# Batch 1's v pooled on GpSimd, and its scores issued in two groups ahead of all its values

## The chip, the cores and the metric

The kernel runs on one core of a Trainium2 chip. The metric is the device time of one execution in microseconds (us), the median of several runs; lower is better. A profile is one further execution, recorded by the hardware profiler: for every instruction it gives the engine, the start, the duration and what released it. PE is TensorE, DVE is VectorE, ACT is ScalarE, POOL is GpSimd, and SP is the engine whose queue starts transposes by DMA and the stores.

## The reference, cut to what matters

Attention over pooled keys and values, followed by an MLP whose activation is `h * cos(h)`:

```python
k_p = k.reshape(B, H, Sp, 8, D).mean(axis=3)          # 576 rows -> 72
v_p = v.reshape(B, H, Sp, 8, D).mean(axis=3)
attn = softmax(q @ k_p.T / sqrt(D))
x = (attn @ v_p)  -> [4608 tokens, 512]               # B=8, H=8, S=576, D=64
h = x @ w_in                                          # 512 -> 2048
out = (h * cos(h)) @ w_out                            # 2048 -> 512
```

All inputs and the output are fp32; the kernel computes in bf16 with fp32 accumulation.

## The kernel before, in words

The 4608 tokens are cut into nine tiles of 512. Tile t has an *up stage* (64 matmuls of 512 columns for h, in eight steps `fp` of 8 matmuls; ACT takes the cosine of each step, DVE multiplies it with h into `g_sb`) and a *down stage* (g times w_out). In tile 0 the down stage is 64 plain matmuls of 512 columns, numbered n = 0 to 63 in an order written out by hand; from tile 1 on it is seven products of 256 columns, built from sums and differences of g (g1 to g4, made by DVE) and of w_out (w1 to w4, made once by `put_weights`). A token tile isn't a batch: a batch has 576 rows, so tile 0 needs the first 512 rows of batch 0, and tile 1 the last 64 of batch 0 and 448 of batch 1. The attention of batch b = t+1 is therefore put between the matmuls of tile t, and its result xT must be there when the up stage of tile t+1 starts.

A manual schedule holds: every engine runs its instructions in the order of the program, and Tile adds the semaphores. So the order of the Python calls is the order on each engine[...].

What the change touches in tile 0:

- **Loads** are issued by POOL's queue, in program order (lines 508 to 522). After batch 0 come w_in 0 to 2, k of batch 1, the first half of q, w_in 3, the second half of q, w_out 0, v, and w_out 2, 1, 3. Batch 1's k and v lie in one staging tile of `kv_st` (two slots), in the *even* layout: 128 partitions with 9 rows each. From batch 2 on, k and v have a layout of their own, 72 partitions with 8 rows of each head, one for each pooled row.
- **Pooling.** In the even layout PE pools with a 0/1 matrix `groups`: `pool_k_mm` (line 170), and `pool_v_mm` (line 181), 18 matmuls and one DVE copy into `vz`, the weights of the values. In the 72-partition layout POOL adds rows: `pool_first` (line 152), four instructions of two heads each into `half_sums`, and `pool_rest` (line 158), two more and a last one into `vz`, or two last ones into `ring` for k.
- **q** is transposed for batch 0 and 1 on PE (`q_transpose_mm`, line 208), 18 blocks, and copied from PSUM by DVE or ACT (line 215).
- **Scores and values.** Batch 1 is cut into four units `us[0..3]`: 256 rows and four heads each, units 0 and 1 for heads 0 to 3, units 2 and 3 for heads 4 to 7. `REST` is the last 64 rows of the batch before, all heads. `scores` is a group of matmuls (line 233) and an exponential on ACT (line 240). `values` (line 262) is a group of matmuls (line 268), then on ACT two logarithms of the sums (line 274) and one exponential (line 275), and then two multiplications on DVE into xT (line 279), which may be put off through a list `later`. These use three PSUM pairs `banks[0..2]`; in tile 0 step fp of the up stage uses `banks[fp % 3]`.
- **The order in the down stage of tile 0** is the list `fill` (line 614): pairs of a matmul number n and what is issued ahead of it.
- **Weights.** `put_weights(i, engine, ks)` (line 381) makes w1 to w4 for half i. DVE makes w1 of half 0 at n = 4, w3 of half 1 at n = 36, and w2 and w4 of half 1 at the end of the stage; POOL makes the others after it has issued the loads of batch 2.
- **Tile 1** needs batch 2: its q and its pooled k are transposed by DMA (`q_transpose`, `k_transpose`, lines 204 and 190, on SP's queue) before the scores, `vz` before `values_rows` (line 287), and the rows of x go through a DMA transpose (line 304) into xT.

In tiles 7 and 8 there is no next batch (`steady` is false). There `reads[1]` takes product 1 out of its PSUM bank (line 447), and product 3 writes that bank again.

The softmax here doesn't subtract the row's maximum and nothing guards it: scores larger than these inputs give would overflow.

## Time and profile before

| | us |
|---|---|
| runs | 286.9, 287.76, 288.06; median 287.76 |
| the profiled execution, device time | 287.52 |
| its span, first to last instruction | 285.7 |
| PE busy | 275.0 (96%) |
| DVE busy | 215.1 |
| ACT busy | 164.2 |
| POOL busy | 144.2 |
| start until tile 0's up stage | 0 to about 16.8 |
| tile 0, up stage | 16.8 to 33.0 |
| tile 0, down stage | 33.0 to 52.65 |
| tile 1 | 52.65 to 83.12 |
| tile 2, as an example of the steady tiles | 83.12 to 112.1 |

Times in the text are from the start of the span. In the chain of work that ended last, each row is a start, a duration and what was at work; a row of DVE, ACT or DMA between rows of PE is a place where PE followed that engine. In the timeline, a row is a start, a duration, the engine, the line of the kernel, the operation, output <- input with partitions x elements, a count, and, in brackets, how long the engine sat idle before and what released it. A duration of merged rows runs from the first start to the last end. The granted clock of TensorE was 0.998, and a matmul of 512 columns was started every 0.216 us (24 of them between 52.65 and 57.83).

### The profile page before, as it was taken

How to read it: one execution, taken by the hardware profiler on the slowest of the kernel's cores; microseconds unless marked ns; L12 is line 12 of the kernel's file. 1: busy time of each engine (PE TensorE's matmuls, PEld its weight loads, DVE VectorE, ACT ScalarE, POOL GpSimd, SP SyncE). 2: the span in 40 equal slices, each digit the busy share in tenths (PEclk: the TensorE clock that was granted, in tenths of full speed). 3: DMA queues.
4: the chain of work that ended last, by engine and by line, in shares of the span. 5: the costliest groups of instructions: out<-in, count | busy, mean ns of one | idle time of the engine just before them, and what ended most of it. 6: DMA issues, size and time to landing. Idle time of an engine off the chain costs nothing.

```text
span 285.7 us, 5835 instructions
## 1 busy us (share of the span) xinstructions
PE 275.0 (96%) x2338; PEld 176.4 (62%) x2360; DVE 215.1 (75%) x314; ACT 164.2 (57%) x193; POOL 144.2 (50%) x150
## 2 busy tenths in 40 slices
PE   7889999999999999999999999999999999999994
PEld 2645554446864697458745874587458845874683
DVE  6458747899947995799569956995699569747972
ACT  3886798367147735773567456745665566337600
POOL 8553079995799359925992499349900000000000
PEclk9999999999999999999999999999999999999999
DMA  7999999795789987897789868882660261015014
GB/s 156 204 207 206 207 205 217 123 181 74 125 109 137 169 172 119 127 179 147 111 135 160 173 97 150 156 176 41 124 147 9 52 137 29 2 36 111 2 37 110
DMA packets 57737, 36.12 MB, mean 126 GB/s; under 512 B 35440, under 2 KB 53360, under 8 KB 57712
## 3 DMA queue, kind: packets, MB, share of 16 engines
q0 software_dynamic: 19744, 18.07, 41.1%
q1 hardware_dynamic: 37328, 17.18, 29.8%
q10 hardware_dynamic: 640, 0.52, 0.8%
q8 instruction: 18, 0.29, 0.4%
q14 instruction: 7, 0.06, 0.1%
HBM read 36.70 MB, written 9.44 MB: 161 GB/s over the span
## 4 chain that ended last, share of the span: by engine, by line
PE 80%; DVE 9%; DMA 3%; ACT 3%; issue 2%; POOL 0%; DVEq 0%; POOLq 0%; ACTq 0%
PE bank L353 35%; PE obank L431 27%; PE obank L370 4%; PE obank L353 4%; DVE g_sb L367 3%; PE bank L233 3%; DVE g L397 3%; DMA q_b<-in_q_dram 2%; ACT cos L363 2%; PE bank L295 2%; DMA xT<-x_rows 1%; PE bank L268 1%; DVE w L387 1%; PE bank L431 1%; ACT ex L240 1%
## 5 line engine op out<-in xcount | busy, mean ns | idle before, releaser
L353 PE MATMUL bank<-xT,w_in_sb 128*128 128x512 bf16 x495 | 113.1, 379 | 1.7 <-DMA xT<-x_rows 0.6
L363 ACT ACTIVATE cos<-bank,half_pi 128x1024 f32<-128x1024 f32 x64 | 70.3, 1113 | 57.7 <-PE bank L353 55.8
L353 PEld LDWEIGHTS <-w_in_sb 128*128 128x128 bf16 x576 | 56.0, 98 | 67.0 <-issue 1.7
L367 DVE TENSOR_TENSOR g_sb<-bank,cos 128x1024 bf16<-128x1024 f32 x64 | 77.3, 1220 | 25.8 <-ACT cos L363 25.6
L156 POOL TENSOR_TENSOR half_sums<-kv_st 72x512 f32<-72x512 bf16 x48 | 54.8, 1167 | 0.7 <-issue 0.2
L240 ACT ACTIVATE ex<-bank 72x1024 bf16<-72x1024 f32 (+1 forms) x40 | 35.0, 928 | 33.9 <-PE bank L233 33.8
L431 PEld LDWEIGHTS <-g 128*128 128x128 bf16 x512 | 47.9, 98 | 7.0 <-issue 1.2
L431 PE MATMUL obank<-w,g 128*128 128x256 bf16 x368 | 42.8, 272 | 0.3 <-DVE p_sb L445 0.2
L431 PEld LDWEIGHTS <-g_sb 128*128 128x128 bf16 x384 | 36.7, 98 | 6.8 <-DVE g_sb L367 0.2
L162 POOL TENSOR_TENSOR half_sums<-half_sums 72x512 f32<-72x512 f32 x24 | 30.4, 1288 | 0.1
L431 PE MATMUL obank<-w_out_sb,g_sb 128*128 128x256 bf16 x240 | 28.8, 273 | 0.0
L397 DVE TENSOR_TENSOR g<-g_sb 128x1024 bf16<-128x1024 bf16 x32 | 23.2, 725 | 0.5
L712 POOL COPY gate<-g 1x1 bf16<-1x1 bf16 x5 | 0.9, 180 | 36.9 <-DVE g L397 36.9
L279 DVE TENSOR_TENSOR xT<-bank,inv 64x256 bf16<-64x256 f32 x14 | 5.9, 422 | 15.1 <-ACT inv L275 15.1
L300 DVE TENSOR_TENSOR x_rows<-bank,inv_rows 128x512 bf16<-128x512 f32 x24 | 16.6, 692 | 0.8
L431 PE MATMUL obank<-w_out_sb,g 128*128 128x256 bf16 x112 | 15.6, 273 | 0.0
L431 PE MATMUL obank<-w,g_sb 128*128 128x256 bf16 x128 | 15.3, 273 | 0.0
L353 PE MATMUL obank<-xT,w_in_sb 128*128 128x512 bf16 x64 | 15.1, 379 | 0.0
L370 PE MATMUL obank<-w_out_sb,g_sb 128*128 128x512 bf16 x61 | 14.7, 379 | 0.4 <-issue 0.3
L233 PE MATMUL bank<-qT,kk 64*72 64x128 bf16 (+2 forms) x288 | 12.8, 221 | 0.1
L233 PEld LDWEIGHTS <-kk 64*72 64x72 bf16 x288 | 8.9, 110 | 5.3 <-issue 3.8
L331 ACT ACT_TABLE_LOAD x9 | 11.5, 1283 | 0.9 <-PEq L730 0.7
(103 smaller groups left out, 276.9 us busy)
## 6 DMA issues: line engine op xcount, KB each, us to landing
out_dram<-o_two SPq DMA_DIRECT2D x64, 128.0 KB, 2.4
kv_st<-in_v_dram POOLq DMA_DIRECT2D x8, 576.0 KB, 11.3
kv_st<-in_k_dram POOLq DMA_DIRECT2D x7, 576.0 KB, 8.3
q_b<-in_q_dram POOLq DMA_DIRECT2D x6, 576.0 KB, 7.7
w_in_sb<-in_moe_w_in_dram POOLq DMA_DIRECT2D x4, 512.0 KB, 13.4
w_out_sb<-in_moe_w_out_dram POOLq DMA_DIRECT2D x4, 512.0 KB, 18.5
q_b<-in_q_dram POOLq DMA_DIRECT2D x4, 288.0 KB, 12.0
g_sb<-in_k_dram SPq DMA_DIRECT2D x1, 576.0 KB, 3.5
```

Source lines behind the costliest of these rows:

```text
L156: nc.gpsimd.tensor_tensor(out=s[:, h:h + 2], in0=x[:, h:h + 2, 0:4, :], in1=x[:, h:h + 2, 4:8, :], op=ADD)
L162: add(out=s[:, h:h + 4, 0:2, :], in0=s[:, h:h + 4, 0:2, :], in1=s[:, h:h + 4, 2:4, :], op=ADD)
L233: nc.tensor.matmul(pair[:Sp, bank, c:c + n].rearrange("p (g n) -> p g n", n=64), lhsT=kk[b % 2][half[r], key_slot(b, h0 + i, r), 0:Sp], rh ...
L240: nc.scalar.activation(out=ex[:, 0:nh * n].rearrange("p (a n) -> p a n", a=2), in_=pair[:Sp, :, 0:nh * n // 2], func=ACTF.Exp, scale=scale ...
L300: nc.vector.tensor_tensor(out=x[0:n].rearrange("p (j a d) -> p j a d", j=KCH, a=2), in0=ps[0:n, :, 0:2 * (D + 2)].rearrange("p j (a w) -> ...
L331: nc.scalar.preload_act_table_set("natural_log_exp_and_others")
L353: nc.tensor.matmul(h[j] if h is obanks else h[:, j, :], lhsT=w_in_sb[fc // 4][:, ki, (fc % 4) * 128:(fc % 4 + 1) * 128], rhs=xT[:, ki, t * ...
L363: nc.scalar.activation(out=c, in_=ps, func=ACTF.Sin, bias=half_pi[:, :1])
L367: nc.vector.tensor_mul(out=o, in0=ps, in1=c)
L370: nc.tensor.matmul(o, lhsT=g_sb[:, fc, ms * 128:(ms + 1) * 128], rhs=w_out_sb[fc // 4][:, fc % 4, :], start=(fc == 0), stop=(fc == FFCH - 1))
L397: nc.vector.tensor_tensor(out=out[:, f0:f1], in0=x, in1=y, op=op)
L431: mms.append(lambda bank=bank, first=first, g=g, w=w, fc=fc, p=p: nc.tensor.matmul(bank[p], lhsT=g(fc, p), rhs=w(fc), start=(first and fc ...
```

## The change

In tile 0:

1. v of batch 1 is loaded in the 72-partition layout, in two DMAs of four heads: one into the second half of batch 1's staging tile, one into the memory of g1, which is otherwise written from tile 1 on. POOL pools it (`pool_first`, `pool_rest`), right after it has issued the loads of k and q of batch 2, and ahead of v of batch 2 and of its `put_weights`. The 18 matmuls and the copy of `pool_v_mm` go.
2. The second half of q of batch 1 is loaded after w_out 2, and its 9 blocks are transposed in the down stage ahead of n = 15 (`late_q`) instead of in step 6 of the up stage. Both copies are DVE's.
3. In `fill`, the scores of REST and of units 0 and 1 come together at n = 8, then the values of REST; the scores of units 2 and 3 together at n = 16; the values of units 0, 1 and 2 together at n = 24, their multiplications at n = 32; the values of unit 3 at n = 44 (before: 40).
4. DVE makes w1 of half 0 after step 5 of the up stage instead of at n = 4.

Elsewhere: in tile 1, POOL issues the next load of k after `pool_rest` of k instead of ahead of it; in tiles 7 and 8, `reads[1]` comes ahead of g3 and g4 of the second half.

```diff
@@ -109,12 +109,16 @@
     def q_tile(b):
         staged["q", b] = qst.tile([128, KCH, ROW, D], BF16, name="q_b", tag="q_b")
 
-    def load_kv(b, which, src):
-
-        st = kv_tile()[:Sp, 0:H * POOL * D].rearrange("p (h t d) -> p h t d", h=H, t=POOL)
-        nc.gpsimd.dma_start(out=st.rearrange("p h t d -> p h (t d)"),
-                            in_=src[b].rearrange("h (p t) d -> p h (t d)", t=POOL))
-        staged[which, b] = st
+    def load_kv(b, which, src, homes=None):
+
+        homes = homes or [kv_tile()]
+        n = H // len(homes)
+        staged[which, b] = []
+        for i, home in enumerate(homes):
+            st = home[:Sp, 0:n * POOL * D].rearrange("p (h t d) -> p h t d", h=n, t=POOL)
+            nc.gpsimd.dma_start(out=st.rearrange("p h t d -> p h (t d)"),
+                                in_=src[b, i * n:(i + 1) * n].rearrange("h (p t) d -> p h (t d)", t=POOL))
+            staged[which, b] += [st[:, h:h + 2] for h in range(0, n, 2)]
 
     def load_q(b):
         q_tile(b)
@@ -151,9 +155,8 @@
 
     def pool_first(b, which):
 
-        x, s = staged.pop((which, b)), half_sums
-        for h in range(0, H, 2):
-            nc.gpsimd.tensor_tensor(out=s[:, h:h + 2], in0=x[:, h:h + 2, 0:4, :], in1=x[:, h:h + 2, 4:8, :], op=ADD)
+        for i, x in enumerate(staged.pop((which, b))):
+            nc.gpsimd.tensor_tensor(out=half_sums[:, 2 * i:2 * i + 2], in0=x[:, :, 0:4, :], in1=x[:, :, 4:8, :], op=ADD)
 
     def pool_rest(b, which):
 
@@ -505,21 +508,27 @@
     half_pi = consts.tile([128, 1], FP32, name="half_pi")
     nc.vector.memset(half_pi, math.pi / 2.0)
 
-    kv_even_tiles(1)
+    st = kv_tile()
+    staged["k", 1] = even_part(st, 0)
     q_tile(1)
     for cg in range(3):
         load_w_in(cg)
     load_even(staged["k", 1], 1, k)
     load_even(staged["q", 1], 1, q, 0, 2)
     load_w_in(3)
-    load_even(staged["q", 1], 1, q, 2, 4)
     load_w_out(0)
-    load_even(staged["v", 1], 1, v)
+    load_kv(1, "v", v, [st[:, KCH * ROW * D:], g1.rearrange("p f n -> p (f n)")])
     nc.gpsimd.memset(vz[1], float(POOL))
     for i in range(2):
         nc.gpsimd.memset(ring[i], 0.0)
-    for cg in (2, 1, 3):
+    load_w_out(2)
+    load_even(staged["q", 1], 1, q, 2, 4)
+    for cg in (1, 3):
         load_w_out(cg)
+    load_kv(2, "k", k)
+    load_q(2)
+    pool_first(1, "v")
+    pool_rest(1, "v")
 
     def warm_up(n, bank):
 
@@ -570,13 +579,14 @@
             if t == 0:
                 if fp == 4:
                     puts = pool_k_mm(1, obanks[0], 0, 2), pool_k_mm(1, obanks[1], 2, 4)
-                elif fp in (5, 6):
-                    g0 = 9 * (fp - 5)
-                    puts = q_transpose_mm(1, obanks[0], g0, g0 + 5), q_transpose_mm(1, obanks[1], g0 + 5, g0 + 9)
-                if fp in (4, 5, 6):
+                elif fp == 5:
+                    puts = q_transpose_mm(1, obanks[0], 0, 5), q_transpose_mm(1, obanks[1], 5, 9)
+                if fp in (4, 5):
                     puts[0](vec)
                     between = ((puts[1], act),)
             up_g(t, fp, between)
+            if t == 0 and fp == 5:
+                put_weights(0, nc.vector, (1,))
             if 0 < t and 3 <= n < 6:
                 put_gs(*[(k, 0) for k in (((3,), (1,), ()) if t == 1 else ((1, 2), (3,), (4,)))[n - 3]])
             if 0 < t and b < B:
@@ -606,15 +616,29 @@
         def V_(n, bank, wait=None):
             return lambda: values(b, us[n], banks[bank], wait)
 
+        def scores_of(*parts):
+            for part in parts:
+                scores_mm(*part)
+            for part in parts:
+                scores_exp(*part)
+
+        def late_q():
+            for put in [q_transpose_mm(1, banks[0][:, i, :], g0, g1) for i, g0, g1 in ((0, 9, 14), (1, 14, 18))]:
+                put(vec)
+
+        def muls():
+            while later:
+                later.pop(0)()
+
         fill = []
         if t < B:
             exp_tables()
             fill = [(1, lambda: scores(t, REST, banks[2])), (16, lambda: values(t, REST, banks[1]))]
         if t == 0:
-            fill = [(2, fill[0][1]), (2, S_(0, 0)), (8, lambda: pool_v_mm(1, banks[1])),
-                    (8, lambda: values(t, REST, banks[2])), (8, S_(1, 0)), (8, V_(0, 1)),
-                    (18, S_(2, 2)), (21, V_(1, 0, later)), (26, S_(3, 1)), (32, lambda: later.pop()()),
-                    (32, V_(2, 2)), (40, V_(3, 0))]
+            fill = [(8, lambda: scores_of((t, REST, banks[2]), (b, us[0], banks[0]), (b, us[1], banks[1]))),
+                    (8, lambda: values(t, REST, banks[2])), (15, late_q),
+                    (16, lambda: scores_of((b, us[2], banks[0]), (b, us[3], banks[1]))),
+                    (24, V_(0, 2, later)), (24, V_(1, 0, later)), (24, V_(2, 1, later)), (32, muls), (44, V_(3, 2))]
         if t == FIRST:
             early_inverses.clear()
         if t < FIRST:
@@ -626,9 +650,7 @@
                 down_mm(obanks[ms % 2], ms, fc)
                 if fc == FFCH - 1:
                     down_out(t, ms, obanks[ms % 2])
-                if n == 4:
-                    put_weights(0, nc.vector, (1,))
-                elif n == 36:
+                if n == 36:
                     put_weights(1, nc.vector, (3,))
             put_weights(1, nc.vector, (2, 4))
         else:
@@ -638,20 +660,9 @@
                 for mm in products[i][j:k]:
                     mm()
 
-            later = []
 
             u0, u1, u2, u3 = [(b, CHUNKS[i], banks[j]) for i, j in enumerate((2, 1, 0, 1))]
             ur = (t, REST, banks[2])
-
-            def scores_of(*parts):
-                for part in parts:
-                    scores_mm(*part)
-                for part in parts:
-                    scores_exp(*part)
-
-            def muls():
-                while later:
-                    later.pop(0)()
 
             steady, rest = b < B, t < B
             if rest:
@@ -667,12 +678,14 @@
                 put_g(2, 0)
             put_gs((1, 1), (2, 1))
             reads[0]()
+            if not steady:
+                reads[1]()
             put_gs((3, 1), (4, 1))
-            reads[1]()
+            if steady:
+                reads[1]()
+                values_rows(*u0)
             if t == 1:
                 put_g(4, 0)
-            if steady:
-                values_rows(*u0)
             product(2)
             reads[2]()
             if steady:
@@ -702,8 +715,6 @@
             sin_tables()
         if b + 1 < B:
             if t == 0:
-                load_kv(b + 1, "k", k)
-                load_q(b + 1)
                 load_kv(b + 1, "v", v)
                 put_weights(0, nc.gpsimd, (3, 2, 4))
                 put_weights(1, nc.gpsimd, (1,))
@@ -711,9 +722,11 @@
 
                 nc.gpsimd.tensor_copy(out=gate, in_=g4[0:1, HF - 1, 0:1])
             pool_first(b + 1, "k")
-            if b + 2 < B:
+            if t != 1 and b + 2 < B:
                 load_kv(b + 2, "k", k)
             pool_rest(b + 1, "k")
+            if t == 1:
+                load_kv(b + 2, "k", k)
             pool_first(b + 1, "v")
 # ---- launch: one core; inputs and outputs as the reference has them ----
 _INS = ['q', 'k', 'v', 'moe_w_in', 'moe_w_out']
```

## The prediction

> **What bounds the kernel now.** First the page's busy times and the table of busy time by stretch: PE is at work nearly always, but in the first down stage (33.00 to 52.70) it leaves 0.7 us open, in tile 1 (52.70 to 83.00) about 1.0, in the last two rows most of what remains.
>
> ```profile
> PE 275.0 (96%) x2338; PEld 176.4 (62%) x2360; DVE 215.1 (75%) x314; ACT 164.2 (57%) x193; POOL 144.2 (50%) x150
> ```
>
> ```profile
> 33.00:52.70 19.70, 19.03 (x129) 9.57 (x131) 12.11 (x18) 16.32 (x23) 15.08 (x11) 1.00 1.11 198
> 52.70:83.00 30.30, 29.33 (x256) 19.36 (x255) 27.32 (x36) 17.03 (x19) 24.67 (x23) 1.00 0.81 121
> ```
>
> (Columns: length, then busy time of PE, PE's weight loads, DVE, ACT, POOL, the clock, DMA share, GB/s.) Then the chain of waits, for the places where PE follows another engine:
>
> ```profile
> 30.97 0.50 PE obank L214 x9
> ...
> 78.77 4.22 DMA xT<-x_rows
> ...
> 246.89 0.61 DVE o_two L447
> ...
> 273.81 0.68 DVE o_two L447 x2
> ```
>
> The first row is the transposes that move: 0.50 us. The DMA is the transpose of x's rows that tile 2 waited for. The other two are the reads of product 1 in tiles 7 and 8. Then the timeline of the first down stage, engine by engine. What matters is the path from REST's exponential to DVE's multiplication:
>
> ```profile
> 35.66 1.50 ACT L240 ACTIVATE ex<-bank 72x512 bf16<-72x512 f32 x2
> 37.21 0.77 ACT L274 ACTIVATE v_sb<-bank 64x256 f32<-64x256 f32 x2
> 38.01 0.42 ACT L275 ACTIVATE v_sb<-v_sb 128x256 f32<-128x256 f32 x1
> ```
>
> ```profile
> 31.29 0.49 DVE L215 COPY qT<-obank 128x640 bf16<-128x640 bf16 x1
> ...
> 38.46 0.86 DVE L279 TENSOR_TENSOR xT<-bank,v_sb 64x256 bf16<-64x256 f32 x2 [0.83 <-ACT v_sb L275]
> ```
>
> Two exponentials, two logarithms and the inverse run one after another on ACT; DVE's multiplications wait for the inverse. The copy of q's transposed blocks is the kind that the change puts behind them.
>
> Lastly POOL's, for its free time and for how late it is afterwards:
>
> ```profile
> 37.13 0.84 POOL L115 DMA_DIRECT2D kv_st<-in_v_dram  x1 [8.28 <-PE bank L185]
> 46.57 4.93 POOL L156 TENSOR_TENSOR half_sums<-kv_st 72x512 f32<-72x512 bf16 x4
> 52.67 2.49 POOL L162 TENSOR_TENSOR half_sums<-half_sums 72x512 f32<-72x512 f32 x2
> 65.14 1.65 POOL L168 TENSOR_TENSOR vz<-half_sums 72x512 bf16<-72x512 f32 x1
> ```
>
> [...] w1 of half 0 (program order n = 4) ran on DVE at 35.52, behind the product of step 7. [...] `put_weights` on DVE took 0.68 us with POOL idle (35.52) and 2.26 us against pooling (53.46). [...] Here k of batch 2 landed 3.7 us after the transfer ahead of it (42.2 to 45.9), v in the even layout 2.8 (31.8 to 34.6)[...], though stores ran beside the former.
>
> **Part by part.** I follow PE.
>
> *Up stage.* Nine transposes go: -0.50, so the down stage starts at 33.04 - 0.50 = 32.54, and n = 8 is due at 32.54 + 8 x 0.216 = 34.27. w1 of half 0 (0.68 us) lies between two g products that DVE waits for anyway (0.38 us idle ahead of 32.15, and the copy of 0.49 us goes), and w_out 0 should land 1.5 us earlier than its 31.8, ahead of the half q: no cost. Without that cover, DVE would be late by 0.7 for `banks[1]` at n = 8.
>
> *n = 8.* ACT's last cosine and table load end 0.50 earlier, so exponentials start at 35.16: REST and unit 0 take 1.50 (36.66), unit 1 some 0.97 (37.63). PE finishes REST's values after REST's own exponential, at about 36.15, then seven matmuls (37.66), nine transposes (38.16), n = 15 (38.38). But now all three exponentials stand ahead of REST's logarithms on ACT: 37.63 + 0.77 + 0.03 + 0.42 = 38.87. REST's multiplications are issued with its values, so on DVE they stand **ahead of both copies of `late_q`**: 38.90 + 0.86 = 39.76, then the copy of five blocks, 0.49, and that of four, an estimate of 0.42 from it: 40.6 with the gaps between. The scores of units 2 and 3 need both copies, for qT and for `banks[0]`. PE therefore waits from 38.38 to 40.65, 2.25 us. This is the step that eats the gain.
>
> *After that.* Two score groups, 0.35 each and 0.2 for the changes of operand (a single group held PE from 40.39 to 40.96): 41.5. Eight matmuls 43.25; three groups of values at 0.44 (as 41.39 to 41.83) 44.57; some 0.1 because `obanks[0]` is read back only 4 matmuls after its last product; 20 matmuls 49.0; unit 3's values 49.4; 20 matmuls 53.75. Before, the stage ended at 52.65: **+1.1**. Included in that is what goes: `pool_v_mm`, 1.17 us on PE, and the 0.7 us of idle time. The exponentials of units 2 and 3 (42.0, 43.0) and the inverses are in time; unit 3's reaches xT at about 53.6, needed at 55.5.
>
> *Loads.* Bytes are the same; v in 72 partitions may cost up to 0.9 us in the stream, below nothing isn't plausible. w_out 2, 1 and 3 landed at 37.2, 39.7, 42.2 and, with the half q moved behind w_out 2, come at 35.6 to 36.5, 39.7 to 40.6, 42.2 to 43.1; they are needed at 36.15, 41.5 and 44.6. Up to 0.35 at the first is swallowed by the later wait. One more DMA in POOL's queue costs it 0.8 us of issue; it waits for DMAs there anyway.
>
> *POOL.* The loads of k and q of batch 2 are issued by about 31 (q waits for an earlier landing, as at 28.08). v pooling: 4 x 1.17 + 2.5 + 1.3 to 1.65 = 8.2 to 8.8, from 31.6 to 40 or 41, needed at 43.25. It fills the 8.28 us wait, but ends later than that did: v of batch 2 is issued at 40.2 instead of 37.13, and four weights, the pooling of k and v are some 3 us late: `ring` at 60.6 (its transposes can't go before q's, at 63 or so, and PE needs them at 69.8), `vz` at 68 to 70, needed at about 72.2. Hidden, with 2 us to spare; each us beyond costs one.
>
> *Tile 1.* DVE's w2 and w4 took 2.26 + 1.65 against POOL's sums of fp32. They now meet the bf16 ones or the pause of a load (w3 took 0.79 beside those): DVE should lose its arrears and PE its wait of 0.21 at 65.11, from the chain. I take -0.2, between +0.3 (w4 blocked again) and -0.4. Tile 1 then ends on PE at 82.52 + 0.9 = 83.4. The transpose that took 4.22 us lands at 82.6 at the latest if everything shifts with PE, and k of batch 4, which was issued at 78.98 beside it, goes behind `pool_rest`, to about 83. So the wait (82.52 to 83.12, 0.60) is covered: tile 2 starts 0.3 late. The later load of k has 20 us until it is pooled.
>
> *Tiles 7 and 8.* The read no longer stands behind two g products: product 3 can follow product 2 at once. In tile 7 product 2 started at 245.52; 16 matmuls of 256 columns at 0.1095 (16 in the 1.75 us from 270.33 to 272.08) end at 247.27, product 3 ran at 247.55: -0.28. In tile 8 product 2 starts at 272.08, so product 3 could at 273.83 and product 4 at 275.58, where the timeline has 276.17: -0.59. g3 is ready two products earlier than needed.
>
> Sum: +1.1 - 0.2 - 0.6 - 0.3 - 0.6 = **-0.6**. Span 285.7 becomes 285.1, the profiled execution 287.52 becomes 286.9. The median shown is 0.24 above that execution: **287.2**.
>
> **The rivals.** *B, the copies aren't held up*, as REST's inverse comes sooner or the copies slip ahead: PE resumes at 38.85, then w_out 1 allows n = 16 between 39.7 and 40.6; gain 0.9 to 1.8 more: **285.7**. For it: all else is balanced[...]. *C, POOL becomes the bound*: it is 3 us late, and `vz` of batch 2 is due at PE's 72.2. Its rows stretch under DVE (1.15 to 1.60 us in line 156; 1.27 to 1.65 in 168). Every row at its longest adds some 2.8, which just reaches PE; only from a further 2.0 (0.6 forecast gain plus 1.44) is it slower than measurable. At a further 3: **289.7**. *D, the small gains don't come*: DVE is blocked again in tile 1, xT is as late as before because v of batch 3, itself 3 us later, crosses the transposes in k's stead, and tile 7 gains nothing: -0.6 + 0.5 + 0.6 + 0.3 = +0.8, **288.6**.
>
> **Numbers.** Likeliest (A) 0.58, own range 286.2 to 288.2; B 0.20; C 0.14; D 0.08. 0.5% is 1.44 us, about what a measurement can tell: 286.3 to 289.2 counts as no change. Of A, 0.05 falls on each side; B gives 0.16 faster; C 0.12 and D 0.04 slower: 0.21 faster, 0.58 same, 0.21 slower. B and C together reach past 2 in 10, so the range runs from inside B to the edge of C: 285.4 to 289.3.
>
> **What would show it.** Right: a PE wait of about 2.2 us ahead of line 233 near 38.4, released by DVE's qT copy, which itself sat behind line 279; the first down stage ending near 53.7; no POOL wait for PE near 28; product 3 right behind product 2 in tiles 7 and 8. Wrong: qT copies ahead of line 279 (B); PE or a POOL gate waiting for line 168 near 72 (C); a wait for xT at tile 2 (D).

## The result, and the profile after

The changed kernel takes 298.41 us (median of 5 runs, 297.89 to 298.71); the kernel before took 287.91 us beside it (5 runs, 286.9 to 288.1). The ratio is 1.0361, 95% interval 1.0331 to 1.039: **slower by 3.6%**, where 287.2 us and "no change" were forecast. The forecast is wrong, and the time lies outside its range of 285.4 to 289.3.

The profiled execution took 298.63 us, its span is 296.8 us (before 287.52 and 285.7). Its stages, read from the timeline of PE (first matmul of each stage), say where the 11.1 us went:

| | before | after | difference |
|---|---|---|---|
| tile 0 ends, tile 1's up stage starts | 52.65 | 55.38 | +2.73 |
| tile 1, up stage (until its first product) | 14.19 | 15.00 | +0.81 |
| tile 1, down stage (until tile 2 starts) | 16.28 | 23.70 | +7.42 |
| tiles 2 to 8 and the end | 202.58 | 202.72 | +0.14 |

Of the first row, 0.35 us lie ahead of tile 0: its up stage starts at 17.14 instead of 16.79. This start differs from profile to profile (16.77 to 17.84 over all kernels here), so a few tenths between the times of two profiles mean nothing by themselves; lengths of stages are safer.

Busy time grew by 3.7 us on PE, 6.0 on DVE and 8.4 on POOL. PE's time without work, span less busy time, grew by 7.4 us (10.7 to 18.1): that is two thirds of the loss.

```profile
PE 278.7 (94%) x2342; PEld 177.5 (60%) x2342; DVE 221.1 (74%) x314; ACT 164.0 (55%) x192; POOL 152.6 (51%) x158
```

The view of waits of PE (total, times, longest, in us) names four that the changed stages have:

```profile
PE obank L434 <- DVE v_sb L450: 5.4, 1, 5.4
...
PE bank L236 <- DVE qT L218: 2.0, 1, 2.0
...
PE bank L356 <- DVE g_sb L370: 1.0, 1, 1.0
...
PE bank L356 <- DMA xT<-x_rows: 0.2, 1, 0.2
```

Only the second of them was in the forecast. The first is the largest, and it stands in tile 1's down stage, where the forecast had seen no change but the load of k. The last is small, but the chain of work that ended last shows that the transpose behind it took 6.78 us (4.22 before), so that it is what sets the start of tile 2:

```profile
87.17 6.78 DMA xT<-x_rows
...
94.08 5.34 PE bank L356 x24
```

**Tile 0.** The timeline of PE (start, duration, with the idle time before and its releaser in brackets):

```profile
40.93 0.63 PE L236 MATMUL bank<-qT,kk 64*72 64x256 bf16 x8 [1.96 <-DVE qT L218]
41.49 2.89 PE L373 MATMUL obank<-w_out_sb,g_sb 128*128 128x512 bf16 x8
```

The last row is eight matmuls of 512 columns. The eight at 32.88 take 1.89 us, and these 2.89. The table of busy time by stretch, with PE's clock as the third number from the end, says why:

```profile
41.00:43.00 2.00, 2.00 (x14) 0.96 (x14) 0.00 (x0) 1.62 (x2) 1.98 (x2) 0.81 1.25 199
43.00:45.00 2.00, 2.00 (x8) 0.96 (x7) 0.00 (x0) 0.31 (x1) 1.92 (x2) 0.50 1.31 207
```

After the wait PE ran at half speed for some 3 us. But this is not what makes the kernel slow: the profiled execution has a mean clock of 0.979 and took 298.63 us, and the two with a mean clock of 0.994 took 298.41 and 297.89. DVE's timeline has the order that the wait comes from, REST's multiplications ahead of the copies:

```profile
39.19 0.86 DVE L282 TENSOR_TENSOR xT<-bank,v_sb 64x256 bf16<-64x256 f32 x2 [3.74 <-ACT v_sb L278]
40.06 0.82 DVE L218 COPY qT<-bank 128x640 bf16<-128x640 bf16 x2
```

**Tile 1's down stage.** DVE's timeline around the longest wait. L400 is `put_g`, and the row of 6.38 us is g4 of the first half (`put_g(4, 0)`), one instruction:

```profile
77.43 0.69 DVE L303 TENSOR_TENSOR x_rows<-bank,inv_rows 128x512 bf16<-128x512 f32 x1
78.03 6.38 DVE L400 TENSOR_TENSOR g<-g_sb,g 128x1024 bf16<-128x1024 bf16 x1
84.34 0.68 DVE L450 TENSOR_TENSOR v_sb<-obank,p_sb 128x512 f32<-128x512 f32 x1
```

The same instruction in the kernel before, on the same engine's timeline:

```profile
73.65 0.68 DVE L397 TENSOR_TENSOR g<-g_sb,g 128x1024 bf16<-128x1024 bf16 x1
```

POOL pools the next k from here on. Ahead of that it copies one element of g4 of the *second* half, its gate: so it can't start before DVE has made that half, which stands a little further ahead on DVE. Before, g4 of the first half began 0.03 us ahead of POOL's first sum (73.65, 73.68). The whole of tile 1 is later now, but what counts is the order of these two: after the change `values_rows(*u0)` stands ahead of g4, and g4 comes 1.07 us *behind* POOL's start (78.03, 76.96):

```profile
76.82 0.18 POOL L723 COPY gate<-g 1x1 bf16<-1x1 bf16 x1 [4.77 <-DVE g L400]
76.96 4.47 POOL L159 TENSOR_TENSOR half_sums<-kv_st 72x512 f32<-72x512 bf16 x4
81.40 2.47 POOL L165 TENSOR_TENSOR half_sums<-half_sums 72x512 f32<-72x512 f32 x2
83.94 1.88 POOL L168 TENSOR_TENSOR ring<-half_sums 72x512 bf16<-72x512 f32 x2
85.77 0.84 POOL L119 DMA_DIRECT2D kv_st<-in_k_dram  x1
```

g4 ends at 84.41, and alone it takes 0.68 us, so it ran only at the very end of its 6.38. Six instructions of POOL, four sums and two more, had gone by without it: the first gap between POOL's rows here is the one of 0.07 us ahead of 83.94. I call this a lockout. The read of product 1 (84.34) is queued behind g4 on DVE, and PE's product waits for the bank that it empties:

```profile
85.07 3.57 PE L434 MATMUL obank<-w,g 128*128 128x256 bf16 x16 [5.39 <-DVE v_sb L450]
```

Sixteen matmuls take 3.57 us here and 1.91 in the same stage at 91.93: the clock was 0.50 from 85 to 89. Then the load of k, issued at 85.77 by POOL's queue, runs beside the transposes of x, which the stall has made late; the chain has 6.78 us for one of them.

**Tiles 7 and 8** went as forecast. In the chain their up stages start at 239.68 and 266.32 (before 228.02 and 254.94, so the difference falls from 11.66 to 11.38), and DVE's last read is at 292.40 (before 281.61, a difference of 10.79). The products of tile 8 follow each other without a gap in the chain:

```profile
283.63 1.75 PE obank L434 x16
285.38 1.75 PE bank L434 x16
...
292.40 0.42 DVE o_two L450
```

### The profile page after: what moved, and what is told of

Its sections match the earlier page's. It is cut to its first block, busy times and chain, and to the rows that moved or that the text cites. A ratio compares the mean times of both kernels' runs of the same rounds, so it can differ in the third digit from the quotient of the medians.

```text
span 296.8 us, 5827 instructions
## 1 busy us (share of the span) xinstructions
PE 278.7 (94%) x2342; PEld 177.5 (60%) x2342; DVE 221.1 (74%) x314; ACT 164.0 (55%) x192; POOL 152.6 (51%) x158
## 4 chain that ended last, share of the span: by engine, by line
PE 63%; DVE 3%; DMA 2%; ACT 0%; issue 0%
PE obank L434 27%; PE bank L356 26%; PE obank L356 3%; PE bank L236 2%; DMA xT<-x_rows 2%; DVE g_sb L370 2%; PE bank L434 2%; PE bank L298 2%; DVE g L400 1%; PE bank L271 1%; ACT cos L366 0%; DVE o_two L450 0%
## 5 line engine op out<-in xcount | busy, mean ns | idle before, releaser
L366 ACT ACTIVATE cos<-bank,half_pi 128x1024 f32<-128x1024 f32 x64 | 70.3, 1113 | 58.1 <-PE bank L356 54.5
L159 POOL TENSOR_TENSOR half_sums<-kv_st 72x512 f32<-72x512 bf16 x50 | 56.5, 1157 | 1.5 <-DMA kv_st<-in_v_dram 1.1
L434 PEld LDWEIGHTS <-g 128*128 128x128 bf16 x512 | 48.7, 99 | 12.6 <-issue 6.1
L434 PE MATMUL obank<-w,g 128*128 128x256 bf16 x368 | 44.5, 279 | 5.6 <-DVE v_sb L450 5.4
L165 POOL TENSOR_TENSOR half_sums<-half_sums 72x512 f32<-72x512 f32 x26 | 32.9, 1285 | 0.1
L400 DVE TENSOR_TENSOR g<-g_sb 128x1024 bf16<-128x1024 bf16 x32 | 23.7, 740 | 0.5
L400 DVE TENSOR_TENSOR g<-g_sb,g 128x1024 bf16<-128x1024 bf16 x16 | 16.6, 1037 | 0.0
L373 PE MATMUL obank<-w_out_sb,g_sb 128*128 128x512 bf16 x64 | 15.9, 397 | 0.0
## 6 DMA issues: line engine op xcount, KB each, us to landing
w_out_sb<-in_moe_w_out_dram POOLq DMA_DIRECT2D x4, 512.0 KB, 18.1
```

The lines of the kernel that those rows point to most:

```text
L159: nc.gpsimd.tensor_tensor(out=half_sums[:, 2 * i:2 * i + 2], in0=x[:, :, 0:4, :], in1=x[:, :, 4:8, :], op=ADD)
L165: add(out=s[:, h:h + 4, 0:2, :], in0=s[:, h:h + 4, 0:2, :], in1=s[:, h:h + 4, 2:4, :], op=ADD)
L366: nc.scalar.activation(out=c, in_=ps, func=ACTF.Sin, bias=half_pi[:, :1])
L373: nc.tensor.matmul(o, lhsT=g_sb[:, fc, ms * 128:(ms + 1) * 128], rhs=w_out_sb[fc // 4][:, fc % 4, :], start=(fc == 0), stop=(fc == FFCH - 1))
L400: nc.vector.tensor_tensor(out=out[:, f0:f1], in0=x, in1=y, op=op)
L434: mms.append(lambda bank=bank, first=first, g=g, w=w, fc=fc, p=p: nc.tensor.matmul(bank[p], lhsT=g(fc, p), rhs=w(fc), start=(first and fc ...
```

## The experiments

My theory after these timelines: (1) g4 was locked out by POOL because the edit put it behind `values_rows(*u0)`; that is most of the loss. (2) What remains comes from the wait for the copies of q, as forecast, and from POOL being late. The rivals: the late g4 is harmful wherever it falls; the moved load of k does it; the wait for q's copies and the clock behind it do the rest.

### g4 in its old place

The changed kernel, g4 put back:

```diff
             if steady:
                 reads[1]()
-                values_rows(*u0)
             if t == 1:
                 put_g(4, 0)
+            if steady:
+                values_rows(*u0)
```

> The changed kernel with one line moved back: in tile 1, g4 of the first half comes ahead of the values of the first 128 rows again, as in the kernel before. Lockout theory (g4[...] now starts after POOL has begun ten pooling instructions without a break, and waits 5.7 us for them): g4 takes about 0.7 us instead of 6.38, tile 1 loses its wait of 5.4 us and what follows it, time 298.4 - 7.4 = about 291, between 290 and 292. Late-POOL rival (pooling v on POOL makes POOL 3.5 us late and the meeting follows from that): the order doesn't matter, g4 or its neighbour is blocked again, time 296 to 299.

Measured: 292.2 us (290.93 to 292.69), ratio 1.0141 (1.0103 to 1.0179), just above the 290 to 292 expected: 6.2 us of the 10.5 are gone. g4 takes 1.46 us here. Tile 0 ends at 53.84, where 53.75 was forecast. The waits that PE has left, in the view of waits:

```profile
PE bank L356 <- DVE g_sb L370: 2.4, 2, 1.2
PE bank L236 <- DVE qT L218: 2.4, 2, 1.9
PE bank L356 <- DMA xT<-x_rows: 1.7, 1, 1.7
```

The first stands in tile 1's up stage, the last ahead of tile 3. So the order of g4 and `values_rows` in this kernel is worth 6.2 us, and some 4 remain.

### A gate that lets POOL start after g4

The changed kernel; in tile 1, POOL's gate reads the first half of g4 and so stays behind it. This takes the collision away by making POOL wait, not by moving DVE's work:

```diff
-                nc.gpsimd.tensor_copy(out=gate, in_=g4[0:1, HF - 1, 0:1])
+                nc.gpsimd.tensor_copy(out=gate, in_=g4[0:1, 0 if t == 1 else HF - 1, 0:1])
```

> The changed kernel with its order kept, but in tile 1 the copy that lets POOL start pooling reads g4's first half instead of the second, so that POOL starts about 1.9 us later, when the late g4 is done. Lockout theory: about 7 us less, 291 to 292, since POOL has time to spare. Order theory (g4 late by itself, no matter what POOL does): no gain, 297 to 299. Late-POOL rival: slower still, 299 to 301.

Measured: 293.8 us (291.0 to 294.9), ratio 1.0216 (1.0175 to 1.0257): well below the change, but above the 291 to 292 expected. In the profiled execution, at 291.0 the fastest of the four, g4 took its own 0.68 us. The order on DVE is that of the changed kernel, so it isn't the place of g4 by itself that costs, but what POOL does meanwhile. The other three executions took 293.44 to 294.9; none of them was profiled, so why is open.

### The late g4 alone, in the kernel before

```diff
             reads[1]()
-            if t == 1:
-                put_g(4, 0)
             if steady:
                 values_rows(*u0)
+            if t == 1:
+                put_g(4, 0)
```

> The kernel before with only this edit: in tile 1, the values of the first 128 rows come ahead of g4 of the first half. POOL still issues the load of k between the fourth and the fifth pooling instruction, a break of about 1.1 us. Lockout theory: g4 waits for the end of the four instructions, about 4 us, and tile 1 loses 3 to 5 us with the slow clock after the wait, time 290.5 to 293. Joint theory (it takes the moved load of k as well): at most 1 us, 287.5 to 289. Late-POOL rival: no change, 287.4 to 288.4.

Measured: 287.86 us (12 runs, 287.4 to 288.52) beside 287.88; ratio 1.0001 (0.9987 to 1.0014). **A miss**: the same edit costs nothing in the kernel before. The timelines of DVE and POOL show the same collision, but a small one:

```profile
75.55 0.88 DVE L397 TENSOR_TENSOR g<-g_sb,g 128x1024 bf16<-128x1024 bf16 x1
```

```profile
74.74 4.93 POOL L156 TENSOR_TENSOR half_sums<-kv_st 72x512 f32<-72x512 bf16 x4 [0.23 <-issue]
```

Here g4 came 0.81 us after POOL had started its first sum (which lasts some 1.1), and got in behind that one. In the changed kernel it came 1.07 us after POOL's start, with the first sum ending at 78.10, and was kept out for all of them. The difference of 0.26 us is in the brackets of POOL's row: between its gate and its first sum POOL has 0.23 us of "issue" here, as in the kernel before, and nothing in the changed kernel. So moving `values_rows` accounts for some 0.84 us of g4's lateness, and this 0.23 us for nearly all the rest. "Late, therefore locked out" was too simple; a few tenths of a microsecond seemed to decide. That had to be tested by itself (the last two experiments).

### The load of k in its old place

```diff
             pool_first(b + 1, "k")
-            if t != 1 and b + 2 < B:
+            if b + 2 < B:
                 load_kv(b + 2, "k", k)
             pool_rest(b + 1, "k")
-            if t == 1:
-                load_kv(b + 2, "k", k)
```

> The changed kernel with the load of k in tile 1 put back between the fourth and the fifth pooling instruction. Lockout theory: g4 gets in at this break, 2.6 us earlier (about 3.9 us instead of 6.38), and k's transfer no longer meets the late transpose of x's rows, time 294 to 296. If the break doesn't matter (g4 needs POOL to finish all): 297.5 to 299.

Measured: 294.72 us (294.38 to 295.51), ratio 1.0239 (1.0207 to 1.0271), as expected. g4 came 1.07 us after POOL's start again, was kept out again, but only until POOL paused to issue the load. It ends at 82.17, so it got in in the gap of 0.30 us ahead of the issue:

```profile
78.21 3.96 DVE L400 TENSOR_TENSOR g<-g_sb,g 128x1024 bf16<-128x1024 bf16 x1
```

```profile
81.91 0.85 POOL L119 DMA_DIRECT2D kv_st<-in_k_dram  x1 [0.30 <-POOL half_sums L159]
```

So the edit that moved the load behind `pool_rest` took away the one break of that size in POOL's work: 3.96 us became 6.38, and 294.72 us became 298.41.

### Both edits in tile 1 undone

The edits of the first and the fourth experiment together; what is left of the change is tile 0 and the last tiles.

> The changed kernel with both edits to tile 1 undone: g4 of the first half ahead of the values, and the load of k between the fourth and the fifth pooling instruction. What is left is tile 0's part and the read in tiles 7 and 8. If g4's lockout was the larger part and the moved load of k the next (in the kernel with g4 moved back, tile 3 still waited 1.75 us for x's transposes, and k of the batch after was loaded across the transposes of q and k): 289.5 to 291, that is 1.5 to 2.5 less than with g4 moved back alone. If the moved load was harmless: 291.5 to 292.5 as there.

Measured: 292.13 us (291.81 to 292.49), ratio 1.0145 (1.013 to 1.016), the same as with g4 alone put back. The theory had expected another 1.5 to 2.5 us, a miss; the rival, that the moved load is harmless, was right: where the load stands moves the wait for x's transposes from tile 3 (1.7 us, above) to tile 2 (1.77 us, below) and gains nothing. The timeline of PE shows what the change in tile 0 costs by itself:

```profile
40.73 0.63 PE L236 MATMUL bank<-qT,kk 64*72 64x256 bf16 x8 [2.17 <-DVE qT L218]
...
61.92 5.34 PE L356 MATMUL bank<-xT,w_in_sb 128*128 128x512 bf16 x24 [1.28 <-DVE g_sb L370]
...
68.45 1.89 PE L356 MATMUL bank<-xT,w_in_sb 128*128 128x512 bf16 x8 [1.19 <-DVE g_sb L370]
...
88.27 5.34 PE L356 MATMUL bank<-xT,w_in_sb 128*128 128x512 bf16 x24 [1.77 <-DMA xT<-x_rows]
```

Tile 0 ends at 53.57, 0.92 later than before. Then PE waits 2.5 us for g in tile 1's up stage, where it had waited 0.21, and 1.77 for x, where it had waited 0.60. The g is late behind w2 on DVE, which took 2.26 us before:

```profile
55.37 3.69 DVE L390 TENSOR_TENSOR w<-w,w_out_sb 128x1024 bf16<-128x1024 bf16 x1
59.09 1.64 DVE L390 TENSOR_TENSOR w<-w_out_sb,w 128x1024 bf16<-128x1024 bf16 x1
```

and POOL at that time is some 3.3 us later in its list than before (52.67 there, 56.00 here, for the sums of fp32):

```profile
49.90 4.93 POOL L159 TENSOR_TENSOR half_sums<-kv_st 72x512 f32<-72x512 bf16 x4
55.13 0.86 POOL L119 DMA_DIRECT2D kv_st<-in_k_dram  x1 [0.30 <-POOL half_sums L159]
56.00 2.50 POOL L165 TENSOR_TENSOR half_sums<-half_sums 72x512 f32<-72x512 f32 x2
58.58 2.33 POOL L168 TENSOR_TENSOR ring<-half_sums 72x512 bf16<-72x512 f32 x2
```

w2 stands at the head of DVE's queue at 55.37, while POOL issues a load, and still runs only at about 58.4 (its end at 59.06 less the 0.68 us that such an instruction takes alone), behind both sums.

### REST's multiplications behind the copies of q

The base is the kernel of the last experiment, as for most of those that follow. This takes away what the copies are queued behind:

```diff
-                    (8, lambda: values(t, REST, banks[2])), (15, late_q),
+                    (8, lambda: values(t, REST, banks[2], later)), (15, late_q), (15, muls),
```

> As tile1_restored, and in tile 0 REST's multiplications on DVE are issued behind the two copies of the late q transposes. Theory of the prediction's stall (copies behind multiplications behind three exponentials): PE's wait near 38.4 shrinks from about 2.2 us to about 0.6, time 1.6 to 3 us less than tile1_restored, depending on how much of the slow clock after the wait goes with it: 287 to 288.5. Rival (PE would wait for w_out instead, since the loads are just in time there): the gain is under 0.8 us.

Measured: 294.93 us (292.86 to 296.3), ratio 1.0236 (1.0188 to 1.0283): slower, a miss. The wait for the copies did shrink, from 2.17 to 0.77 us, so they had been held up by the multiplications. But tile 0 ends at 53.34, only 0.23 earlier (0.48 if counted from the start of its up stage), since PE ran into the weights:

```profile
39.58 0.63 PE L236 MATMUL bank<-qT,kk 64*72 64x256 bf16 x8 [0.77 <-DVE qT L218]
...
44.19 4.56 PE L373 MATMUL obank<-w_out_sb,g_sb 128*128 128x512 bf16 x20 [0.75 <-DMA w_out_sb<-in_moe_w_out_dram]
...
88.48 7.95 PE L356 MATMUL bank<-xT,w_in_sb 128*128 128x512 bf16 x24 [3.64 <-DMA xT<-x_rows]
```

And in tile 1 the transposes of x made PE wait 3.64 us, after which it ran slowly (7.95 us for 24 matmuls that take 5.34; the clock was 0.75 from 84 to 90 and 0.68 from 90 to 96). So a PE that is earlier in tile 0 gained nothing here.

### Matmuls in the wait

Nine matmuls whose result nobody uses, ahead of n = 16, to keep PE busy while it waits for the copies:

```diff
-                    (16, lambda: scores_of((b, us[2], banks[0]), (b, us[3], banks[1]))),
+                    (16, lambda: warm_up(9, banks[1][:, 0, :])), (16, lambda: scores_of((b, us[2], banks[0]), (b, us[3], banks[1]))),
```

> As tile1_restored, with nine matmuls without use (512 columns, some 1.9 us) put on PE into the wait ahead of n = 16, into a bank that is free. If the granted clock falls because PE stood still for 2 us there: the clock of the profile stays at 1.00 and the spread of the times closes at the low end, 0 to 1.5 us less than tile1_restored. If the clock has another cause: no change or up to 0.3 us more.

Measured: 292.96 us (292.6 to 294.99), ratio 1.0188 (1.0152 to 1.0224): 0.8 us more, where at most 0.3 more was expected. It doesn't tell what the clock is worth: the kernel without them had a clock of 1.00 behind its wait of 2.17 us in its profile, so there was nothing to win back in that execution. That the slow clock isn't in every execution is plainer from three profiles with a wait of 2.0 us there: the change (1.96 us) has a clock of 0.50 from about 42.3 to 45.7 behind it, the kernels of w1 on DVE (mean clock of the execution 1.0) and of one copy more (1.00 from 40 to 46), both below, don't.

### w2 and w4 of half 1 among the steps of tile 1

From the kernel with REST's multiplications behind; the two come after steps 2 and 3 of tile 1's up stage instead of ahead of it:

```diff
+            if t == 1 and n in (2, 3):
+                put_weights(1, nc.vector, (2 * n - 2,))
...
-            put_weights(1, nc.vector, (2, 4))
```

> As rest_muls_behind_q, and DVE makes w2 and w4 of the second half in tile 1 behind the third and the fourth g product instead of at the end of tile 0, where they waited for POOL's sums (2.58 + 1.64 us, in another run 3.70 + 1.64, and PE then 1.0 to 2.4 us for g products). Lockout theory: both take 0.7 to 1.3 us there, beside POOL's first sums of v, PE's waits for g products in tile 1 go, and the time falls by 1 to 2.5 us below rest_muls_behind_q, to 285 to 287. If DVE was only short of time in tile 1: no change within 0.5 us.

Measured: 293.8 us (292.72 to 297.87), ratio 1.0203 (1.0164 to 1.0242), where 285 to 287 was expected, a miss. It is 1.1 us below its base, within the spread of the two. w2 takes 1.46 us and w4 1.75 there, so they do better; but the g of the last step is then queued behind them, and PE waits 2.41 us for it. And a weight holds up tile 0 at its second place:

```profile
41.88 1.89 PE L373 MATMUL obank<-w_out_sb,g_sb 128*128 128x512 bf16 x8 [1.54 <-DMA w_out_sb<-in_moe_w_out_dram]
...
68.72 1.89 PE L356 MATMUL bank<-xT,w_in_sb 128*128 128x512 bf16 x8 [2.41 <-DVE g_sb L370]
```

### v of batch 1 back on PE

From the kernel with tile 1 restored. v is loaded in the even layout and pooled by `pool_v_mm`; the order of scores and values, the late half of q and the early w1 stay (units 0 and 1 exchange places, for their banks):

```diff
...
-    load_kv(1, "v", v, [st[:, KCH * ROW * D:], g1.rearrange("p f n -> p (f n)")])
+    load_even(staged["v", 1], 1, v)
...
-    pool_first(1, "v")
-    pool_rest(1, "v")
...
-            fill = [(8, lambda: scores_of((t, REST, banks[2]), (b, us[0], banks[0]), (b, us[1], banks[1]))),
+            fill = [(8, lambda: pool_v_mm(1, banks[0])),
+                    (8, lambda: scores_of((t, REST, banks[2]), (b, us[1], banks[1]), (b, us[0], banks[0]))),
```

> As tile1_restored, but v of batch 1 is loaded in the even layout and pooled on PE again, at n = 8 ahead of the scores (into bank pair 0, so the scores of units 0 and 1 change places). The order of scores and values and the wait for the q copies stay. Late-POOL theory (POOL is 3.5 us late with everything that it does after v, so DVE's w2 meets its sums, and the loads of batch 3 meet the transposes of x's rows): DVE's w2 and w4 and PE's waits for g products and for x's transposes return to what the kernel before shows, time 287.5 to 289.5. Rival (the new order in the first down stage, with PE's wait of 2 us there, costs the 4 us by itself): 291 to 293.

Measured: 289.06 us (7 runs, 288.83 to 289.96), ratio 1.0044 (1.0026 to 1.0061), within what the theory of a late POOL expected. PE has 1.17 us more to do in tile 0 and ends it at 54.70 instead of 53.57 (0.67 of this is a later start of the up stage), and the kernel is still 3.1 us faster. The gain stands in the two stages after it, tile 1's up stage (15.54 us against 16.61) and its down stage (15.53 against 18.09; no wait for x). POOL had waited until PE had used the staging tile, and was free again earlier:

```profile
36.63 0.84 POOL L119 DMA_DIRECT2D kv_st<-in_v_dram  x1 [7.48 <-PE bank L236]
...
52.75 2.50 POOL L165 TENSOR_TENSOR half_sums<-half_sums 72x512 f32<-72x512 f32 x2
```

Here too POOL has its 0.23 us of "issue" behind the gate, and g4 is 0.02 us ahead of the sums (77.07, 77.09) and takes 0.68 us, against 1.46 in the base; PE's wait of 0.5 us for the read behind it (in the base) is part of the 3.1. Collisions are not gone, though: w3 at 52.47 takes 3.34 us, and PE waits 1.6 us for xT behind it.

### w1 of half 1 on DVE

The other way to relieve POOL, again from the kernel with tile 1 restored: one of its four weights goes to DVE, at n = 20 of tile 0.

```diff
-                if n == 36:
+                if n == 20:
+                    put_weights(1, nc.vector, (1,))
+                elif n == 36:
                     put_weights(1, nc.vector, (3,))
...
                 put_weights(0, nc.gpsimd, (3, 2, 4))
-                put_weights(1, nc.gpsimd, (1,))
```

> As tile1_restored, but w1 of half 1 is made by DVE ahead of n = 20, where DVE has nothing to do, instead of by POOL: POOL gains 2.1 of its 3.5 us back. Late-POOL theory: w2 meets other instructions of POOL, and the wait for x's transposes shrinks, 1 to 3 us less than tile1_restored: 289 to 291. Rival (order in the first down stage): within 0.7 us of tile1_restored, 291.5 to 292.8.

Measured: 290.96 us (290.88 to 291.65), ratio 1.0107 (1.0087 to 1.0127), 1.2 us better, within what was expected. v stays on POOL, POOL's sums of fp32 start 1.4 us earlier (54.62, where 2.1 was expected), w2 takes 2.59 us in place of 3.69, and PE's wait for g falls to 1.1 us; the wait for x stays at 1.62. Less lateness of POOL gives less loss: two different ways, the same direction. How much of it comes through w2 and how much through the transposes of x isn't separated.

### The reads at the end, alone

The kernel before, with nothing of the change but the order in tiles 7 and 8:

```diff
             reads[0]()
+            if not steady:
+                reads[1]()
             put_gs((3, 1), (4, 1))
-            reads[1]()
+            if steady:
+                reads[1]()
```

> The kernel before with only the earlier read of product 1 in tiles 7 and 8. The prediction's step: -0.28 - 0.59, so 0.9 us less than the kernel before run beside it, 0.6 to 1.1. If the end is bound by something else than that read (the stores): no change.

Measured: 287.1 us (19 runs, 286.77 to 287.92) beside 287.9 (27 runs); ratio 0.9973 (0.9964 to 0.9982). A gain of 0.8 us, where the prediction's step has 0.28 + 0.59.

### The ends and the later load of k

The same, with the load of k of tile 1 behind `pool_rest` as in the change:

```diff
-            if b + 2 < B:
+            if t != 1 and b + 2 < B:
                 load_kv(b + 2, "k", k)
             pool_rest(b + 1, "k")
+            if t == 1:
+                load_kv(b + 2, "k", k)
```

> As ends_alone, and in tile 1 the load of k behind pool_rest, as in the changed kernel. If that load only stood in the way of x's transposes, the wait of 0.60 us ahead of tile 2 goes: 0.3 to 0.7 us less than ends_alone. If it only moves the collision to the transposes of q and k in tile 2, or takes the break out of POOL's work that DVE needs: no gain or up to 2 us more.

Four of its six executions took 286.33 to 286.84 us (ratio 0.9949, 0.993 to 0.9968), and two took 294.36 and 295.09; the median of the six is 286.77. In the profiled one PE did not wait for x at tile 2 (0.60 us before). The median of the four is the lowest here, but a kernel that sometimes takes 8 us more isn't the better one. Neither of the two was profiled, so their cause isn't shown; the kernel before had one execution of that kind too, 292.08 us, in the 15 that ran beside the first four experiments. The ends alone are what I would keep.

### POOL a fraction of a microsecond later

The test of the phase. The changed kernel with all its orders; POOL merely repeats its gate copy of one element in tile 1, so that it starts its sums later while DVE's order stays:

```diff
-                nc.gpsimd.tensor_copy(out=gate, in_=g4[0:1, HF - 1, 0:1])
+                for _ in range(2 if t == 1 else 1):
+                    nc.gpsimd.tensor_copy(out=gate, in_=g4[0:1, HF - 1, 0:1])
```

> The changed kernel with one more one-element copy on POOL ahead of the pooling in tile 1, about 0.14 us. Phase theory (g4 gets in behind POOL's first instruction if it asks well before that one ends, and misses all later ones if it asks as it ends; in the changed kernel it asked 1.07 us after a start of 1.12 us): asking 0.93 us after the start, at the edge: g4 takes either some 0.9 us, time 291 to 293, or 6.3 us again, 298; it may differ from run to run. Order theory (g4 behind POOL's start always waits for a break): 298 to 299.

Measured: 291.47 us (291.2 to 291.99), ratio 1.0131 (1.0112 to 1.015). **6.9 us gained by one more instruction.** The timelines of DVE and of POOL:

```profile
77.91 0.86 DVE L400 TENSOR_TENSOR g<-g_sb,g 128x1024 bf16<-128x1024 bf16 x1
```

```profile
76.69 0.42 POOL L724 COPY gate<-g 1x1 bf16<-1x1 bf16 x2 [4.77 <-DVE g L400]
77.08 4.93 POOL L159 TENSOR_TENSOR half_sums<-kv_st 72x512 f32<-72x512 bf16 x4
```

g4 comes 0.83 us after POOL's start and takes 0.86 us, as in the kernel before with the late g4.

And with three copies more:

```diff
-                nc.gpsimd.tensor_copy(out=gate, in_=g4[0:1, HF - 1, 0:1])
+                for _ in range(4 if t == 1 else 1):
+                    nc.gpsimd.tensor_copy(out=gate, in_=g4[0:1, HF - 1, 0:1])
```

> The same with three more copies, about 0.42 us: g4 asks 0.65 us after POOL's start. Phase theory: it gets in behind the first pooling instruction as in the kernel before with the late g4 (0.81 us after the start, g4 took 0.88 us): g4 takes about 1.1 us, time 291 to 293.5. Order theory: g4 takes about 6.8 us, 298.4 to 299.

Measured: 292.07 us (290.7 to 293.17), ratio 1.0163 (1.0133 to 1.0192); g4 comes 0.36 us after POOL's start and takes 1.33 us:

```profile
77.64 1.33 DVE L400 TENSOR_TENSOR g<-g_sb,g 128x1024 bf16<-128x1024 bf16 x1
```

The profiles in one table (start of g4 minus start of POOL's sums, both from the timelines; the first sum lasts some 1.1 us). The kernel with the gate on g4 is left out, since POOL starts behind g4 there.

| kernel | g4 after POOL's start, us | g4 takes, us |
|---|---|---|
| before; the ends alone, and with the load of k; v back on PE | -0.03 to -0.02 | 0.68 |
| g4 in its old place; tile 1 restored, and the four others from it | 0.23 to 0.24 | 1.46 |
| three copies more | 0.36 | 1.33 |
| kernel before, g4 late | 0.81 | 0.88 |
| one copy more | 0.83 | 0.86 |
| load of k in its old place | 1.07 | 3.96 |
| the change | 1.07 | 6.38 |

Ahead of POOL it runs at once, in 0.68 us. From 0.23 to 0.83 us behind POOL's start it waits for about the end of the first sum and runs: the two columns add up to 1.69 to 1.70 us in each of these rows, so the later it comes, the less it waits. At 1.07, some 0.07 us ahead of that end, it misses the end and all later ones up to a gap between POOL's rows (0.30 us in the first case, 0.07 in the second).

The table is for this one meeting of g4 and POOL's sums, and its limit isn't a rule for others. In the change's own profile another g instruction came 0.04 us ahead of the end of a sum (65.70) and got in one sum later (that one ends at 66.92, the g instruction at 67.47):

```profile
65.66 1.81 DVE L400 TENSOR_TENSOR g<-g_sb 128x1024 bf16<-128x1024 bf16 x1
```

And w2 in the kernel before (shown in the next section) came 0.49 us ahead of such an end and missed it. That tenths of a microsecond decide is shown; by what rule is not.

## Why the prediction was wrong

Two steps failed, both about DVE and POOL. The order of g4 and `values_rows` in tile 1 was put at nothing, by not being mentioned: it costs 6.2 us. And the later POOL was taken to be hidden: it costs 2.9. By ratio to the kernel before, times its 287.9 us, the difference is made up so, with the edits undone in this order: 6.2 us from tile 1 (1.0361 to 1.0145; g4 put back alone gives the same), 2.9 from v on POOL (1.0145 to 1.0044), 2.0 left over for the rest of the change in tile 0 (1.0044 to 0.9973), less 0.8 from the ends. In the order of the prediction:

- **Up stage, -0.50.** Right: it takes 15.74 us (17.14 to 32.88) instead of 16.25 (16.79 to 33.04). That the down stage starts at 32.88 instead of the forecast 32.54 comes from the later start.
- **n = 8, the wait of 2.25 us.** Right, and with the releaser and the order on DVE that it named: 1.96 us in the change, 2.17 with tile 1 restored. That DVE took its instructions in the order of the program carried it: the copies ran at 40.06, behind REST's multiplications (39.19 to 40.05), and moving the multiplications behind the copies took 1.4 us of the wait away (2.17 to 0.77).
- **After that, end of tile 0 at 53.75.** Right to some 0.4 us where the clock held (53.57 and 53.84, from starts 0.14 and 0.48 later), and 1.6 short in the change's own profile (55.38), where PE ran at half speed behind the wait. No step allowed for the clock. It was 0.50 behind a wait of 1.96 us in the change's profile, and stayed at 1.00 behind 2.0 in two others (w1 on DVE, one copy more) and behind 2.17 in a third (tile 1 restored). So the length of this wait alone didn't decide it, and what it costs differs from one profile to the next.
- **Loads.** w_out 1 and 3 were put at 40.6 and 43.1 at the latest. With REST's multiplications behind the copies, PE got there sooner and waited until 44.19 for one of its w_out groups (the one needed at n = 24), in the kernel built on it until 41.88 for the one needed at n = 16: 1.1 and 1.3 us later than the latest estimates. It didn't matter for the likeliest case, but it takes rival B away: with most of the hold-up gone, tile 0 ended less than 0.5 us earlier.
- **POOL, "Hidden, with 2 us to spare". This step failed.** Its times were right to within a microsecond: v pooled by 40.7, `vz` at 70.3, and PE waits for neither. (Its terms for pooling v add up to 8.5 to 8.8 us, not 8.2 to 8.8, which changes nothing.) But I asked only whether POOL is late for PE. The prediction itself had `put_weights` on DVE at 0.68 us beside an idle POOL and 2.26 us beside its sums, and 3 us of lateness changed what DVE's w2 met (3.69 us with tile 1 restored). With v back on PE 3.1 us came back although PE had 1.2 more to do. The price of the step is +2.9, with PE's saving already counted in, where nothing was put for it.
- **Tile 1, "-0.2, between +0.3 and -0.4". Failed in sign and size.** w2 was to meet bf16 sums or the pause of a load. With tile 1 restored it did come in the pause, at 55.37, and took 3.69 us: PE waits 2.5 us for g instead of none. In the change itself, with tile 0 late by the clock, w2 took 2.58 us and the wait was 1.03; so this term depends on when PE gets there.
- **The step that is missing, and that most of the loss comes from.** The diff also puts `values_rows(*u0)` ahead of `put_g(4, 0)` in tile 1. The prediction reads that part of the diff only for tiles 7 and 8 (`reads[1]`), and the list of changes at the top leaves it out as well. A full list would have had: two of DVE's instructions go ahead of g4 of the first half, while POOL's gate hangs on g4 of the second half as before; so g4, which was ahead of POOL's sums by 0.03 us, falls behind their start by 0.81, as in the kernel before with the late g4; the other 0.26 up to the 1.07 measured go with POOL's 0.23 us of "issue", which the diff doesn't show. The prediction had one such meeting from the profile, w2 with 2.26 us where w1 took 0.68. From it a wait of 1.6 us would have followed, an estimate (2.26 - 0.68), not 5.7 (6.38 - 0.68): one meeting gave no cause to expect that DVE is passed over six times. Measured: +6.2 us, with what follows from it (PE waits 5.39 us, runs at half clock after it, and the transposes of x then lie beside the load of k).
- **The moved load of k, covered.** With g4 in its old place it neither costs nor gains (292.2 us with it, 292.13 without), but in the change it removed the break that would have let g4 in after 3.96 us.
- **Tiles 7 and 8, -0.28 and -0.59.** Right to the hundredth in the profile, and -0.8 alone in the kernel before.
- **The rivals.** C named POOL but as a bound for PE, which it never was (and its 289.7 isn't what its terms give: 287.2 and 3 are 290.2). D had DVE blocked again in tile 1, for 0.5 us; none had more. That the range was narrow followed from this: nothing that DVE could lose had been counted at more than 0.5 us.

For the step that is missing, the profile before gave a hint, in the 2.26 us of w2 that the prediction quotes. w2 came 0.49 us ahead of the end of the first of two sums of fp32, and ended at 55.72, so it was passed over at that end and ran behind the second (POOL's next row starts at 55.24):

```profile
53.46 2.26 DVE L387 TENSOR_TENSOR w<-w,w_out_sb 128x1024 bf16<-128x1024 bf16 x1
```

```profile
52.67 1.28 POOL L162 TENSOR_TENSOR half_sums<-half_sums 72x512 f32<-72x512 f32 x1
```

What stays open: what decides between getting in and being passed over, for g4 somewhere between 0.83 and 1.07 us, elsewhere otherwise; what makes the 0.23 us of "issue" on POOL that is there in the kernels with v pooled on PE and not in the others; why the clock falls behind a wait of 2 us in tile 0 in the change's profile and not in three others; the three slower executions with the gate on g4; and the 294 to 295 us that two executions of the ends with the later load took.

## What to carry to other kernels

When work moves to GpSimd, ask what the new time of its instructions does to DVE's beside them (here w1 took 0.68 us beside an idle GpSimd, w2, of the same size, 2.26 and 3.69 us beside its sums, and g4 6.38), and not just whether GpSimd meets its deadlines; allow for a collision with a whole run of back-to-back GpSimd instructions (six here), not with one. Read a diff's moved lines one by one, each on each engine: the line that cost most here was a reordering of two calls. And when the same edit is harmless in one kernel and costs 6 us in another, shift one side by a few tenths of a microsecond and see: that was a change of one line here, and the clearest experiment.

## What the runs showed of the hardware that I had not expected

- A DVE instruction of 0.68 us took 6.38 us beside six POOL instructions without a gap, and 0.86 us when it came 0.24 us sooner after POOL's start: here it was passed over at every boundary between them, not only held up by the one that ran.
- Whether a DMA issue on POOL lets DVE in differs. g4 got in in the gap of 0.30 us ahead of an issue (3.96 us instead of 6.38). w2 with tile 1 restored, which came 0.24 us into the issue of 55.13 to 55.99, got in only behind the two sums that followed it. A g instruction of the kernel before, also 0.24 us into an issue (94.68, in 94.44 to 95.27), took its 0.68 us at once.
- PE's clock was 0.50 behind 1.96 us without work in one profile (the change), and 1.00 behind 2.0 us in two others (w1 on DVE, one copy more) and behind 2.17 us in a third (tile 1 restored).
